# Counting the result's store on a semaphore outside the Tile context

## The chip, the cores and the metric

The kernel runs on one core of a Trainium2 chip. The metric is device microseconds of one execution; the runs of the kernel before gave 377.08, 377.2 and 377.08 us, so the median is 377.08 us. One execution was recorded by the profiler. It took 377.07 us itself; the span that the profile covers, from the first instruction to the last, is 375.3 us of that.

Engine names are those of the profile: PE is TensorE, PEld its weight loads, DVE VectorE, ACT ScalarE, POOL GpSimd, SP SyncE. A name with a q behind it (SPq, POOLq) is that engine's instruction queue, where semaphore and DMA-issuing instructions run.

## The reference

Two input rows `x` of 512 numbers are normalised, and three things are added: the row itself, sliding attention over the last 2048 keys and values of a cache of 32 heads, and a bilinear gated layer. Cut to what matters:

```
xn = layernorm(x)                                   # x: 2 x 1 x 512
q  = xn @ wq                                        # 32 heads of 128
k, v = k_cache[:, :, 6144:, :], v_cache[:, :, 6144:, :]
p  = softmax(q @ k^T / sqrt(128))                   # 2 x 32 x 1 x 2048
a  = (p @ v) @ wo                                   # 2 x 512
b  = ((xn @ w_gate) * (xn @ w_up)) @ w_down         # 512 -> 1376 -> 512
return x + a + b
```

Everything is float32. The kernel returns one tile of 128 x 128 numbers, which are the 2 x 512 results in rows 0, 1, 32, 33, 64, 65, 96 and 97; the other rows hold nothing that is read.

## The kernel before, in words

All inputs are packed on the host into one long array, `stream`, in the order in which the kernel wants them. The Sync engine pulls it in pieces of up to 31 x 512 numbers a partition into three rotating buffers named `step`; a buffer is asked for again when its last field was used. The keys of a head are multiplied by the query and summed on DVE (`products`, `sums`), the softmax is made with ACT and POOL (`maxima`, `weights`, `reciprocals`), and PE multiplies probabilities by values (`weigh`) and the outcome by `wo` (`project_o`). The gated layer's products (`project_gu`, `gate`, `down`) are spread between the heads. All of it adds up in one PSUM tile, `acc`.

Each engine's instructions are kept in the order in which the code issues them (the class `InOrder` ties each to the one before it on its engine); the Tile context inserts the semaphores. Each DMA that the context sees is counted on one of eight semaphores in turn, DMAHW0 to DMAHW7, and before a semaphore is used again the queue waits for its previous count.

The end of the program is what the change touches. After the last multiplication of `down_half`, DVE copies `acc` to the SBUF tile `o_out` (L591), and Sync stores `o_out` to DRAM (L593). Then the `with` statement of L692 ends, and the Tile context closes. In the built program its closing consists of these steps, all with line L692 in the profile:

- On Sync, five waits, each for two semaphores, which together hold every DMA semaphore and those of DVE and ACT at their last values, then a drain that waits for POOL's. The fourth of the five holds DMAHW6, on which the store counts, at 64.
- A first barrier over all five engines: PE, DVE, ACT and Sync each drain and count up one semaphore, POOL waits for four counts and then raises a second semaphore, for which each of the four waits.
- On POOL, a drain and one instruction that clears the context's twelve semaphores.
- A second barrier of the same form. Nothing of the kernel's stands behind it.

PE, DVE, ACT and POOL issue their first drain as soon as their own work is done, and stand there until Sync has come through its waits.

`PADS` sets two tiles that nothing reads or writes. They only shift the addresses of the others.

Of the kernel before, what the change touches and what calls it, by code (L numbers as in the profile page):

```python
# [8 lines left out]
F32 = mybir.dt.float32  # L9
# [7 lines left out]
P = 128  # L17
# [12 lines left out]
OUT = P  # L30
# [15 lines left out]
TG = [(0, 5), (32, 3), (32 + 3 * OWN, 1)]  # L46
TR = [OWN, OWN, FT - 8 * OWN]
TP = TG[-1][0] + TR[-1]
PADS = 608, 248


def k(h):
# [94 lines left out]
def kernel(  # L147
# [2 lines left out]
    tail: bass.AP,  # L150
    stream: bass.AP,
    out: bass.AP,
):
    nc = tc.nc
    pe, dve, act, sp = (InOrder(tc, e) for e in (nc.tensor, nc.vector, nc.scalar, nc.sync))
# [3 lines left out]
    const = ctx.enter_context(tc.tile_pool(name="const", bufs=1))  # L159
# [5 lines left out]

    const.tile([P, PADS[0]], F32, name="pad0")
    wd_tail = const.tile([TP, D], F32, name="wd_tail")
# [61 lines left out]
    acc, acc_g = acc_t[:M, :], acc_t[:, :P]  # L229
# [173 lines left out]
    def project_o(h):  # L403
        wo = got["wo", h][0]
        if h < HF:
            pe.matmul(acc, oT.pop(h), wo, start=(h == 0), stop=False)
        else:
            accumulate(oT.pop(h), wo)
        done("wo", h)
# [66 lines left out]
    def down_half(c, n):  # L476
        w = got["wh", (c, n)][0]
        for g in range(4):
            pe.matmul(
                acc_g[32 * g : 32 * g + M, n * HP : (n + 1) * HP], hT[:, c % 4, c // 4, :],  # L480
                w[:, g * HP : (g + 1) * HP], start=False, stop=(c, n) == (NFC - 1, 1),
            )
        done("wh", (c, n))
# [99 lines left out]
    project_o(H - 1)  # L583
    down(3)
    project_o(H - 2)
    o_out = const.tile([P, P], F32, name="o_out")
    const.tile([P, PADS[1]], F32, name="pad1")
    for c in range(WD[-1][1], NFC):
        for n in range(2):
            down_half(c, n)  # L590
    dve.tensor_copy(o_out, acc_g)  # L591

    sp.dma_start(out, o_out[:OUT, :])  # L593


def laid_out(x):
# [100 lines left out]
```

## Time and profile before

| what | value |
|---|---|
| median of the runs | 377.08 us |
| the profiled execution's own time | 377.07 us |
| its span, first to last instruction | 375.3 us |
| DVE busy | 294.5 us, 78% |
| PE busy | 256.5 us, 68% |
| HBM read | 159.47 MB |
| DMA, share of the chain that ended last | 60% |
| last copy, `o_out` from `acc`, begins | 372.53 us |
| store of `o_out` issued | 372.85 us |

The last row but one and the last place the change: everything that it touches lies in the 2.4 us between the issue of the store and the end of the span. The view by line of the profile gives the instructions of L692, the closing of the context, with durations in ns and the first and last start in us. The time outside the span, 377.07 less 375.3, is not covered by any record of an instruction.

### The profile page before, as it was taken

What the parts mean: (1) busy time and instruction counts of PE and PEld (TensorE: products, weight loads), DVE (VectorE), ACT (ScalarE), POOL (GpSimd) and SP (SyncE); (2) the same over time, 40 slices, a digit from 0 to 9 for tenths busy, and PEclk for the clock granted to TensorE, in tenths of its full rate; (3) what the DMA queues carried; (4) which work ended last, traced back from release to release, by engine and by line L of the source; (5) the groups of instructions that cost most, each with busy time, mean ns of one, the idle gap of its engine ahead of it and who ended that gap; (6) DMA issues with size and microseconds to landing.
All of it is one profiled execution on the core that took longest, in us unless ns stands there. A gap on an engine that the chain in (4) does not pass through costs nothing.

```text
span 375.3 us, 2897 instructions
## 1 busy us (share of the span) xinstructions
PE 256.5 (68%) x1108; PEld 89.7 (24%) x1108; DVE 294.5 (78%) x144; ACT 57.4 (15%) x260; POOL 25.6 (7%) x75
## 2 busy tenths in 40 slices
PE   3167695884586852685858805887546757699996
PEld 3133122231222220222222202222111212133343
DVE  3069999369989369999269999794699999999750
ACT  1002011110210210021012002111100211112131
POOL 1000000000000000000000000010000001000010
PEclk9999897888586996689868965898865988689899
DMA  8999999999999999999999999999999999999995
GB/s 344 419 438 479 452 407 440 433 433 434 435 427 433 433 433 433 435 426 433 433 433 436 440 433 433 447 436 420 433 440 433 435 433 433 433 433 407 419 415 230
DMA packets 4088, 159.70 MB, mean 426 GB/s; under 512 B 458, under 2 KB 714, under 8 KB 1132
## 3 DMA queue, kind: packets, MB, share of 16 engines
q1 hardware_dynamic: 4076, 159.54, 98.5%
q8 instruction: 8, 0.13, 0.1%
q14 instruction: 4, 0.03, 0.0%
HBM read 159.47 MB, written 0.07 MB: 425 GB/s over the span
## 4 chain that ended last, share of the span: by engine, by line
DMA 60%; PE 23%; DVE 14%; ACT 1%; issue 1%; SPq 0%; DVEq 0%
DMA step<-in_stream_dram 60%; PE o_ps L131 8%; DVE s L131 7%; DVE step L131 7%; PE q L131 7%; PE acc L131 5%; PE tr L131 3%; ACT o_sb L131 1%; ACT oT L131 0%; DVE m L131 0%; SPq L131 0%; DVE o_out L131 0%; DVE rec L131 0%; DVEq L131 0%
## 5 line engine op out<-in xcount | busy, mean ns | idle before, releaser
L131 DVE TENSOR_TENSOR step<-step,q 128x4096 f32<-128x4096 f32 x31 | 136.8, 4412 | 44.5 <-DMA step<-in_stream_dram 41.0
L131 DVE TENSOR_REDUCE s<-step 128x32 f32<-128x4096 f32 x32 | 141.4, 4419 | 1.1
L131 PE MATMUL o_ps<-step,p 128*16 128x512 f32 x512 | 77.7, 665 | 44.8 <-DMA step<-in_stream_dram 44.8
L131 PE MATMUL q<-step,xnb 128*128 128x512 f32 (+1 forms) x128 | 76.9, 748 | 33.9 <-DMA step<-in_stream_dram 33.9
L131 PEld LDWEIGHTS q<-step,xnb 128*128 128x128 f32 x128 | 29.3, 247 | 85.1 <-issue 69.2
L131 PE MATMUL acc<-step,oT 128*2 128x512 f32 (+1 forms) x88 | 38.0, 591 | 8.6 <-ACT oT L131 8.6
L131 PE MATMUL tr<-first,o_sb 128*128 128x2 f32 (+4 forms) x192 | 28.7, 268 | 17.1 <-ACT o_sb L131 11.8
L131 PEld LDWEIGHTS o_ps<-step,p 128*16 128x16 f32 x512 | 14.1, 100 | 96.6 <-DMA step<-in_stream_dram 53.7
L131 PEld LDWEIGHTS tr<-first,o_sb 128*128 128x128 f32 (+2 forms) x192 | 26.0, 208 | 42.4 <-ACT o_sb L131 35.0
L131 ACT COPY o_sb<-o_ps 128x512 f32<-128x512 f32 x23 | 13.5, 586 | 144.5 <-PE o_ps L131 144.5
L328 POOL PARTITION_ALL_REDUCE mm<-m x32 | 11.4, 357 | 242.9 <-DVE rec L131 137.6
L131 ACT ACTIVATE nm<-mm 128x2 f32<-128x2 f32 x32 | 6.6, 205 | 129.1 <-POOL mm L328 129.1
L131 ACT ACTIVATE p<-s,nm 128x16 f32<-128x16 f32 x64 | 19.2, 300 | 1.0
L344 POOL PARTITION_ALL_REDUCE sum<-rs x32 | 12.7, 398 | 94.7 <-ACT p L131 94.7
L131 PE MATMUL o_ps<-step,xn 128*2 128x512 f32 (+1 forms) x48 | 13.5, 618 | 5.6 <-DMA step<-in_stream_dram 5.6
L131 ACT ACTIVATE oT<-tr,rec 128x1 f32<-128x1 f32 x64 | 12.1, 260 | 26.9 <-PE tr L131 26.9
L131 DVE TENSOR_TENSOR step<-step,tr 128x4096 f32<-128x4096 f32 x1 | 4.4, 4420 | 15.0 <-DMA step<-in_stream_dram 15.0
L131 ACT ACTIVATION_READ_ACCUMULATOR p<-s,nm 128x1 f32 x64 | 11.9, 187 | 0.0
L131 PE MATMUL q<-xnb,mean_w 128*128 128x512 f32 (+4 forms) x26 | 11.5, 553 | 0.0
L131 PEld LDWEIGHTS acc<-step,oT 128*2 128x2 f32 x88 | 4.4, 88 | 22.0 <-ACT oT L131 12.1
L131 DVE RECIPROCAL rec<-sum 128x2 f32<-128x2 f32 x32 | 5.0, 155 | 4.3 <-POOL sum L344 4.3
L131 DVE COPY o_out<-acc 128x128 f32<-128x128 f32 x1 | 0.3, 292 | 8.5 <-PE acc L131 8.5
(42 smaller groups left out, 49.6 us busy)
## 6 DMA issues: line engine op xcount, KB each, us to landing
step<-in_stream_dram SPq DMA_DIRECT2D x15, 7936.0 KB, 35.5
step<-in_stream_dram SPq DMA_DIRECT2D x1, 7808.0 KB, 38.8
step<-in_stream_dram SPq DMA_DIRECT2D x1, 7680.0 KB, 20.9
step<-in_stream_dram SPq DMA_DIRECT2D x1, 7552.0 KB, 57.2
step<-in_stream_dram SPq DMA_DIRECT2D x1, 4864.0 KB
step<-in_stream_dram SPq DMA_DIRECT2D x1, 3328.0 KB, 18.9
step<-in_stream_dram SPq DMA_DIRECT2D x1, 2304.0 KB, 24.0
step<-in_stream_dram SPq DMA_DIRECT2D x2, 1024.0 KB, 16.2
```

The lines of the kernel that those rows point to most:

```text
L131: made = call(*args, **kwargs)
L328: nc.gpsimd.partition_all_reduce(mm, m, P, bass_isa.ReduceOp.max)
L344: nc.gpsimd.partition_all_reduce(sum_t[h], rs, P, bass_isa.ReduceOp.add)
```

## The change

The tile `o_out` is taken outside the Tile context, by the plain SBUF allocator, and lies at another address; the two pads are resized by 128 numbers each, so that every other tile keeps its address. The store keeps its place behind the copy by a dependency that is added by hand, is taken out of the context's own counting, and counts on a semaphore of its own, `stored`. The context's closing therefore no longer holds the store; its wait for DMAHW6 goes to 48, the count of the DMA before. Behind the closing, Sync waits for `stored` to reach 16 and clears it. In the built program these two are one instruction, a clear that carries the wait.

```diff
-PADS = 608, 248
+PADS = 480, 376
...
-    o_out = const.tile([P, P], F32, name="o_out")
     const.tile([P, PADS[1]], F32, name="pad1")
...
-    dve.tensor_copy(o_out, acc_g)
-
-    sp.dma_start(out, o_out[:OUT, :])
+    last = dve.tensor_copy(o_out, acc_g)
+    store = sp.dma_start(out, o_out)
+    tc.add_manual_dep(
+        store.ins, last.ins.name,
+        mybir.DependencyInfo(mybir.DependencyClass.Sync, mybir.DependencyReason.DATA),
+        reason="the result",
+    )
+    tc.no_tile_sem_insts.add(store.ins.name)
+    store.then_inc(stored, 16)
...
+    o_out = nc.alloc_sbuf_tensor("o_out", [P, P], F32).ap()
+    stored = nc.alloc_semaphore("stored")
     with _tile.TileContext(nc) as tc:
-        tile_sliding_attention_plus_glu_kernel(tc, *args)
+        tile_sliding_attention_plus_glu_kernel(tc, *args, o_out, stored)
+    nc.sync.wait_ge(stored, 16)
+    nc.sync.sem_clear(stored)
```

On PE, DVE, ACT and POOL every instruction and every wait stands where it stood. On Sync, the piece of the difference at the end of the program is this (`out_dram` is the result, the names in brackets are the semaphores waited for since the row before, and waits without an instruction of their own are gathered into the next row):

```order
 L131 DMA step<-in_stream_dram 128x512
 L131 DMA step<-in_stream_dram 128x256
-L131 DMA out_dram<-o_out 128x128 [waits DMAHW6_49,DVE_49]
-L692 UNCONDITIONAL_BRANCH
+L131 DMA out_dram<-o_out 128x128 [waits DVE_49]
+L701 UNCONDITIONAL_BRANCH
+L704 ISA [waits DMAHW3_49,DMAHW2_49,DMAHW4_49,DMAHW1_49,DMAHW5_49,DMAHW0_49,DMAHW6_49,DVE_49,DMAHW7_49,Activation_49,Pool_49,barrier_Pool_Activation_PE_DVE_SP_release,stored]
```

The store lost its wait for DMAHW6, the closing lost none of its waits, and one instruction, the clear with its wait for `stored`, stands behind the closing's last barrier. With the wait that went and the clear that came, Sync has 68 instructions in both programs.

More of the change, by code (lines that the diff above doesn't have):

```diff
@@ L152 @@
     out: bass.AP,
+    o_out: bass.AP,
+    stored,
 ):
@@ L691 @@
         args.append(nc.dram_tensor(f"out_{i}_dram", shape, dt, kind="ExternalOutput").ap())
+    o_out = nc.alloc_sbuf_tensor("o_out", [P, P], F32).ap()
+    stored = nc.alloc_semaphore("stored")
     with _tile.TileContext(nc) as tc:
-        kernel(tc, *args)
+        kernel(tc, *args, o_out, stored)
+    nc.sync.wait_ge(stored, 16)
+    nc.sync.sem_clear(stored)
     r = _run(nc, [arrays], core_ids=[0])
```

## The prediction

> **What bounds the kernel, and what of it the change can reach.** I read the page first, for the shape of the whole.
>
> ```profile
> span 375.3 us, 2897 instructions
> DMA  8999999999999999999999999999999999999995
> q1 hardware_dynamic: 4076, 159.54, 98.5%
> DMA 60%; PE 23%; DVE 14%; ACT 1%; issue 1%; SPq 0%; DVEq 0%
> ```
>
> The DMA engines are busy nine tenths of nearly every slice and hold 60% of the chain that ended last. The loading of keys and values bounds the kernel, and only the last slice thins out. None of that is touched, since all five engines run the same instructions in the same order up to the store. So the question is what happens in the last slice. The instructions in order of time show how it ends:
>
> ```profile
> 371.83 0.63 PE L131 MATMUL acc<-step,hT 128*2 128x64 f32 x32
> 372.53 0.29 DVE L131 COPY o_out<-acc 128x128 f32<-128x128 f32 x1 [8.53 <-PE acc L131]
> 372.85 0.35 SPq L131 DMA_DIRECT2D out_dram<-o_out  x1
> ```
>
> PE ends, DVE copies, Sync issues the store at 372.85, and no engine computes any more. What Sync waits for from 372 us on is told by the view of its own waits (us in total, times, longest):
>
> ```profile
> SPq L131 <- DVE o_out L131: 18.0, 1, 18.0
> SPq L692 <- DMA out_dram<-o_out: 1.0, 1, 1.0
> SPq L692 <- PEq L692: 0.6, 2, 0.4
> ```
>
> In the closing (L692) Sync stands 1.0 us for the store to land, and then 0.6 us in two waits of the barriers. So the closing is paid behind the store. I cut the end into stretches at the instants found below, from the store's issue to the span's end (length, then busy time and count of PE, PEld, DVE, ACT, POOL, then clock, DMA share, GB/s):
>
> ```profile
> 372.85:373.20 0.35, 0.00 (x0) 0.00 (x0) 0.00 (x0) 0.00 (x0) 0.00 (x0) 1.00 0.00 0
> 373.20:373.69 0.49, 0.00 (x0) 0.00 (x0) 0.00 (x0) 0.00 (x0) 0.00 (x0) 1.00 0.00 0
> 373.69:374.05 0.36, 0.00 (x0) 0.00 (x0) 0.00 (x0) 0.00 (x0) 0.00 (x0) 1.00 0.60 182
> 374.05:374.40 0.35, 0.00 (x0) 0.00 (x0) 0.00 (x0) 0.00 (x0) 0.00 (x0) 1.00 0.00 0
> 374.40:375.28 0.88, 0.00 (x0) 0.00 (x0) 0.00 (x0) 0.00 (x0) 0.00 (x0) 0.71 0.00 0
> ```
>
> The store is issued in 0.35 us, 0.49 us pass before its first packets, these move for 0.36 us, and 0.35 us more pass before Sync sees the count, 1.55 us in all. Then 0.88 us of closing follow.
>
> The instants come from the instructions of L692 (counts, then ns least/median/most, first and last start). The first row is Sync's from 373.2 to 373.45; the second is Sync's from 373.4 to 374.42; the rest are all engines' from 374.75 on:
>
> ```profile
> L692 SPq EVENT_SEMAPHORE  x3: 28/28/28, 373.2 to 373.4; - x3
> ...
> L692 SPq EVENT_SEMAPHORE  x1: 27/27/27, 374.4 to 374.4; - x1
> ...
> L692 POOLq DRAIN  x2: 34/58/82, 374.8 to 375.0; - x2
> ...
> L692 POOLq EVENT_SEMAPHORE_RANGE_CLEAR  x1: 96/96/96, 374.9 to 374.9; - x1
> ...
> L692 SPq EVENT_SEMAPHORE  x1: 17/17/17, 375.2 to 375.2; - x1
> ...
> L692 PEldq EVENT_SEMAPHORE  x1: 51/51/51, 375.2 to 375.2; - x1
> ```
>
> Three of Sync's five closing waits pass at once; in windows of 0.02 to 0.03 us the first lies at 373.25 and the third at 373.38, so they follow each other by about 0.065 us. The fourth, which holds the store, runs only at 374.40 (it alone lies between 374.39 and 374.41). Sync leaves the last barrier in a row of 17 ns that lies at 375.21 to 375.24, and PE in the row of 51 ns, in which the span ends: it is the only one of L692 running at 375.27 and none is left at 375.285, so I put the end at 375.28.
>
> **The change part by part.**
>
> 1. The store's wait for DMAHW6 goes. Sync stood 18.0 us there for DVE's copy (the first row of its waits), so the earlier wait passed inside that time. Worth nothing; without that cover it would be one passed wait, 0.03 to 0.065 us by the rows above. The copy is still what the store waits for, so the issue stays at 372.85.
>
> 2. `o_out` has another address. No row shows this copy or store at two addresses. The nearest are POOL's first fills, two of one shape at two addresses:
>
> ```profile
> L678 POOL MEMSET const-float32-0.0<- x1: 98/98/98, 0.2 to 0.2; 128x1 f32 x1
> L678 POOL MEMSET const-float32-1.0<- x1: 99/99/99, 0.3 to 0.3; 128x1 f32 x1
> ```
>
> They differ by 1 ns of 98, which on the copy's 0.29 us and the store's 0.36 us of packets is under 0.01 us, to either side. I take nothing. The pads hold every other tile in place.
>
> 3. The closing no longer waits for the store. Its fourth wait passes about 0.065 us behind the third, at 373.45 instead of 374.40, which is 0.95 us earlier (the row of waits says 1.0). All that follows it, 0.88 us, moves by as much: the last barrier ends at 375.28 - 0.95 = 374.33, and Sync is through it at 375.24 - 0.95 = 374.29. The other four engines wait for Sync alone there: each came to its first drain when its work was done, DVE with its copy last of all, by the row of its two drains in the closing (the first from 372.5, 330 ns long):
>
> ```profile
> L692 DVEq DRAIN  x2: 19/174/330, 372.5 to 374.9; - x2
> ```
>
>
> 4. Behind the closing Sync waits for `stored`. The store is seen at 374.40 as before, for nothing of its 1.55 us changes. Sync is there 0.11 us early, so the store and not the closing ends last. That is the new wait: nothing is queued behind it on Sync but the end of the program, and no other engine waits for it. If the closing took 0.11 us longer than here, the cover would be gone and each further 0.1 us would be paid.
>
> 5. The clear of `stored` is new on the path. No row shows a clear on Sync. The same instruction on POOL took 0.096 us for twelve semaphores; Sync's plain semaphore instruction in the same place took 0.017 us. It clears one semaphore, so it lies between the two, and I take the middle, 0.06 us. The dearest instruction that Sync has here, the issue of the store, took 0.35 us, and is the far end.
>
> The sum: 374.40 + 0.06 = 374.46 for the end of the span, against 375.28, a gain of 0.82 us. The ends by the nearer rows are 0.86 us (0.017) and 0.78 us (0.096), by the far one 0.53 us. The profiled execution took 377.07 us, so 376.25; the median of the runs is 0.01 above it, which gives 376.26 us, or 0.22% less. The bound above which a measurement of this kernel tells a change from none is 0.2%, 0.75 us, so the forecast clears it by 0.07 us only.
>
> This assumes that the 1.79 us outside the span (377.07 - 375.28) stay as they are and begin when the last engine is through. No row shows what happens in them. The Trainium skill, page "Runtime: NRT & Kernel Launch", section "The ~15µs preamble/postamble breakdown", says that after the kernel there is first a barrier that waits for all engines, of about 1.5 us, and only then the resetting of semaphores; by that rule Sync's late clear sets the end and the gain is the 0.82 us of the sum. The page's stages behind the kernel add up to about 5 us, which is more than the 1.79 us that this case leaves for all that is outside, so I don't take it as settled.
>
> **The rivals.**
>
> *Only four engines count.* If what follows the span begins on each engine by itself and Sync is not the one that it ends on, Sync's 0.11 us of waiting and its clear are hidden, and the gain is the whole shift of part 3, 0.95 us: 376.13 us. For it speaks that four engines of five are released at 374.33; against it, that all five left the barrier together before, so nothing shows which one is waited for.
>
> *The new end is dearer.* The clear on Sync costs as much as the dearest row, 0.35 us: the span ends at 374.75, the gain is 0.53 us, and the time is 376.55 us, no change that can be told. The same comes of 0.29 us more anywhere between the landing and the end. For it speaks that POOL's clear took more than five times its plain semaphore instruction, with a drain of its own ahead; against it, that Sync's drains and waits all took 7 to 28 ns. It decides from a clear of 0.13 us on (0.82 - 0.75 + 0.06).
>
> *Slower: the added instruction is not at hand.* The clear stands behind the place at which Sync's program ended. Were it to be fetched from memory when Sync comes to it, at 374.29, the fetch would stand bare. Its price is bounded by these rows, the fetches by their queue (packets, MB, share of 16 engines) and the first load of the kernel (KB, us from issue to landing):
>
> ```profile
> q8 instruction: 8, 0.13, 0.1%
> ...
> first<-in_stream_dram SPq DMA_DIRECT2D x1, 271.0 KB, 2.9
> ```
>
> A packet of instructions took about 0.001 x 16 x 375.3 / 8 = 0.75 us of one engine; a whole load took 2.9 us. With 2.9 us the span ends at 374.29 + 2.9 + 0.06 = 377.25 and the time is 379.04 us. It turns slower from a fetch of 0.93 us on (375.28 - 374.29 - 0.06), and by 0.2% from 1.68 us. Against it: Sync has 68 instructions before and after, and before, it passed its whole closing in steps of 0.065 us with no hole but the store's.
>
> That the change does not do what it says is not open: in the built program the closing's wait for DMAHW6 is at 48 now, the count before the store's.
>
> **How the numbers follow.** The likeliest is the sum, 0.58, with its own range from 376.15 to 376.40: the two nearer ends, 376.22 and 376.30, widened by the 0.1 us by which the runs before differ (377.08 to 377.2). Only four engines count: 0.18. A dearer end: 0.20, spread between 376.33 and 376.7. The fetch: 0.04. The range 376.05 to 376.60 holds the first two and most of the third. Faster by over 0.2% means under 376.33: all of the second and 0.50 of the first, since its margin of 0.07 us is less than the scatter of the runs: 0.68. Within 0.2%: the other 0.08 of the first and the third, 0.28. Slower: the fetch, 0.04.
>
> **What would show it.** In the changed kernel's profile: up to the store's issue at 372.85 nothing moves by more than runs do. Part 3 is right if Sync's five closing waits follow each other without the hole of 1.0 us, and the other engines' last rows of the closing lie near 374.3. Part 4 is right if Sync's waits name the store once more, behind the closing, with some 0.1 us. Part 5 is right if a clear on Sync of 20 to 100 ns ends the span at 374.4 to 374.5. If the span shrinks by 0.82 us and the time by another amount, the assumption on what lies outside is wrong. What would make the forecast wrong most easily is a store that lands later than 374.40: nothing covers it now, and each 0.1 us of it goes to the end as it did before.

## The result, and the profile after

The changed kernel takes 376.12 us (median of 10 runs, 376.03 to 376.30), the kernel before 377.12 us beside it (10 runs, 376.92 to 377.26). The ratio is 0.9974, with a 95% interval from 0.9964 to 0.9983: faster by 1.00 us of the medians, about a quarter of a percent. Forecast were 376.26 us and a gain of 0.82 us, within 376.05 to 376.60. The profiled execution took 376.18 us itself.

The page of the changed kernel has as many instructions as before, the same queue of loads and the same chain:

```profile
span 374.5 us, 2897 instructions
q1 hardware_dynamic: 4076, 159.54, 98.7%
DMA 60%; PE 23%; DVE 14%; ACT 1%; issue 1%; SPq 0%; DVEq 0%
```

The end in order of time, and then Sync's waits from 370 us on:

```profile
372.61 0.29 DVE L131 COPY o_out<-acc 128x128 f32<-128x128 f32 x1 [8.53 <-PE acc L131]
372.93 0.35 SPq L131 DMA_DIRECT2D out_dram<-o_out  x1
```

```profile
SPq L131 <- DVE o_out L131: 18.1, 1, 18.1
SPq L701 <- PEq L701: 0.6, 2, 0.4
```

The copy and the issue take what they took, 0.29 and 0.35 us, and come 0.08 us later than in the profile of before, less than the 0.34 us by which the runs of the kernel before differ here (376.92 to 377.26). The row of 1.0 us in which the closing waited for the store is gone. The closing's instructions (L701 now), in the view by line, are the same in number, and within 10 ns in length:

```profile
L701 SPq EVENT_SEMAPHORE  x7: 17/28/28, 373.3 to 374.3; - x7
L701 PEldq EVENT_SEMAPHORE  x2: 51/51/51, 373.9 to 374.3; - x2
L701 POOLq EVENT_SEMAPHORE_RANGE_CLEAR  x1: 96/96/96, 374.0 to 374.0; - x1
```

In the part from 373.2 to 373.7 us Sync's five closing waits now stand together, where before the fourth was at 374.4:

```profile
L701 SPq EVENT_SEMAPHORE  x5: 28/28/28, 373.3 to 373.6; - x5
```

And the new instruction, the clear on Sync that carries the wait for `stored`, in the view of its line:

```profile
L704 SPq EVENT_SEMAPHORE_RANGE_CLEAR  x1: 30/30/30, 374.5 to 374.5; - x1
```

The same stretches as before, cut at this profile's instants (issue; to the last packet; to the end of the wait for `stored`; the clear):

```profile
372.93:373.28 0.35, 0.00 (x0) 0.00 (x0) 0.00 (x0) 0.00 (x0) 0.00 (x0) 1.00 0.00 0
373.28:374.12 0.84, 0.00 (x0) 0.00 (x0) 0.00 (x0) 0.00 (x0) 0.00 (x0) 1.00 0.27 78
374.12:374.49 0.37, 0.00 (x0) 0.00 (x0) 0.00 (x0) 0.00 (x0) 0.00 (x0) 1.00 0.00 0
374.49:374.52 0.03, 0.00 (x0) 0.00 (x0) 0.00 (x0) 0.00 (x0) 0.00 (x0) 1.00 0.00 0
```

The store takes 1.56 us from issue to seen (1.55 before), then 0.03 us of clear follow in the place of 0.88 us of closing. From the store's issue to the end of the span there were 375.28 - 372.85 = 2.43 us, and there are 1.59 us now: 0.84 us less, where the sum had 0.82. PE's last row of the closing ends at 374.40 (found in a narrow window, as before), 0.12 us ahead of the span's end.

One number does not fit the sum. The time less the span was 1.80 us on average over 35 runs of the kernel before (each run lists its span to 0.1 us), and is 1.70 us over these 10 runs. A tenth of a microsecond was gained where no instruction is recorded. That is what most of the experiments are about.

### The profile page after: what moved, and what is told of

Read it like the earlier page. It is cut to its first block, busy times and chain, and to the rows that moved or that the text cites. A ratio compares the mean times of both kernels' runs of the same rounds, so it can differ in the third digit from the quotient of the medians.

```text
span 374.5 us, 2897 instructions
## 1 busy us (share of the span) xinstructions
PE 260.7 (70%) x1108; PEld 90.3 (24%) x1108; DVE 294.5 (79%) x144; ACT 57.2 (15%) x260; POOL 25.6 (7%) x75
## 4 chain that ended last, share of the span: by engine, by line
DMA 60%; PE 23%; DVE 14%; ACT 1%; issue 1%; SPq 0%; DVEq 0%
DMA step<-in_stream_dram 60%; PE o_ps L131 8%; DVE s L131 7%; DVE step L131 7%; PE q L131 7%; PE acc L131 5%; PE tr L131 3%; ACT o_sb L131 1%; ACT oT L131 0%; DVE m L131 0%; SPq L131 0%; DVE o_out L131 0%; DVE rec L131 0%; DVEq L131 0%
## 5 line engine op out<-in xcount | busy, mean ns | idle before, releaser
L131 PE MATMUL q<-step,xnb 128*128 128x512 f32 (+1 forms) x128 | 78.7, 763 | 35.4 <-DMA step<-in_stream_dram 35.4
L131 PE MATMUL acc<-step,oT 128*2 128x512 f32 (+1 forms) x88 | 39.7, 612 | 8.6 <-ACT oT L131 8.6
```

What stands on the lines that cost most here:

```text
L131: made = call(*args, **kwargs)
```

## The experiments

All are edits of the changed kernel, timed beside the kernel before. The time less the span is called *the rest* from here on; its mean over a kernel's runs repeats to about 0.02 us from session to session: it was 1.78 to 1.80 us for the kernel before in the three sessions of these experiments, and 1.70 and 1.68 us for the changed kernel in two.

**The address alone.** The store goes back to the context's counting; the tile stays outside.

```diff
-    tc.no_tile_sem_insts.add(store.ins.name)
-    store.then_inc(stored, 16)
...
-    nc.sync.wait_ge(stored, 16)
-    nc.sync.sem_clear(stored)
```

> The tile o_out lies outside the context and the pads are resized, as in the changed kernel, but the store counts on the context's own semaphore again and nothing waits behind the closing. Theory (the gain comes of the closing running beside the store): the closing waits for the store again, Sync stands about 1.0 us in its fourth wait, and the time is that of the kernel before, 377.1 us within 0.1. Rival (the address of o_out or the pads give part of the gain): 376.1 to 376.9 us, with a shorter copy or store.

Measured: 377.18 us, a ratio of 0.9998 (0.9990 to 1.0007) to the kernel before. Sync's waits have the store again:

```profile
SPq L698 <- DMA out_dram<-o_out: 1.0, 1, 1.0
```

So the address and the pads give nothing, and the whole gain hangs on where the store is waited for.

**Sync ends later.** Sixteen clears of an unused semaphore on Sync, behind its clear of `stored`. The semaphore `idle` is added in the same way in the other runs with clears.

```diff
+    idle = nc.alloc_semaphore("idle")
...
     nc.sync.sem_clear(stored)
+    for _ in range(16):
+        nc.sync.sem_clear(idle)
```

> The changed kernel with 16 more clears of an unused semaphore on Sync behind its clear of stored; at about 0.065 us each, the step of Sync's closing waits, Sync ends 1.0 us later, span 375.5 us. Theory of the sum (what lies outside the span begins when the last engine is through): the whole of it is paid, 377.1 to 377.2 us, and time less span stays at 1.7 us. Rival (only four engines count, Sync has slack outside the span): less is paid than the span grows, so that time less span falls; with a slack of 0.5 us 376.6 us, with one of 1.0 us or more 376.1 us.

Measured: 377.28 us. The clears in the view of their line:

```profile
L707 SPq EVENT_SEMAPHORE_RANGE_CLEAR  x16: 25/30/49, 374.5 to 375.9; - x16
```

The span is 376.0 us, 1.5 us longer than the changed kernel's, and the time rose by 1.16 us from its 376.12. The rest fell from 1.70 to 1.31 us. Four tenths of Sync's lateness were not paid: Sync has a slack outside the span, and the assumption that what follows begins with the last engine is wrong for Sync. (Part of the 1.31 us may be a transfer behind the span, of which more below; the next run has none.)

**Sync ends a little later.** The same with four clears, small enough to fit into that slack.

```diff
     nc.sync.sem_clear(stored)
+    for _ in range(4):
+        nc.sync.sem_clear(idle)
```

> The changed kernel with 4 more clears on Sync, 0.06 us each as the 16 of the earlier run, so that Sync ends at 374.75 and with it the span. New theory (Sync has slack outside the span: the time is the later of the other engines' end, 374.40, plus 1.80 us, and of Sync's end plus 1.31 us): the first is 376.20, the second 376.06, so the time does not move from the changed kernel's 376.12 us by more than 0.1, and time less span falls to 1.45 us. Rival (the last engine's end counts, with 1.70 us outside): 376.4 us, time less span 1.7 us.

Measured: 376.26 us, the span 374.8 us, the rest 1.44 us. The clears end the span 0.25 us behind where it would have ended:

```profile
L705 SPq EVENT_SEMAPHORE_RANGE_CLEAR  x1: 30/30/30, 374.5 to 374.5; - x1
L707 SPq EVENT_SEMAPHORE_RANGE_CLEAR  x4: 25/28/39, 374.6 to 374.8; - x4
```

The rest fell by 0.26 us, as much as the clears took. The median lies 0.14 us over the changed kernel's first measurement, a little more than the 0.1 us expected, and 0.04 us over its second (376.22 us, below). On the kernel before in the same session (377.17 us) it gains 0.91 us, where the changed kernel gained 1.00 and 0.93 us: so the clears cost 0.02 to 0.09 us, against the 0.25 us that they would have had to. The rival's 376.4 us and 1.70 us did not come. This small lateness of Sync costs nothing that can be told from the scatter.

**Another barrier.** One more barrier of all engines between the closing and the wait.

```diff
+    nc.all_engine_barrier()
     nc.sync.wait_ge(stored, 16)
```

> The changed kernel with one more barrier of all engines between the closing and Sync's wait for stored. A barrier of the closing took 0.33 to 0.48 us there. Theory (the store ends last, with the closing's end 0.1 to 0.15 us ahead of it): the cover is used up and only the rest is paid, 0.2 to 0.35 us: span 374.7 to 374.9, 376.3 to 376.5 us, and Sync no longer waits for stored. Rival (the closing ended last, or its cover is larger): all of it, 376.45 to 376.6 us, or nothing, 376.1 us.

Measured: 376.61 us, the rest 1.79 us. Sync's waits and PE's row of the new barrier:

```profile
SPq L703 <- PEq L703: 0.3, 1, 0.3
...
L703 PEldq EVENT_SEMAPHORE  x1: 51/51/51, 374.8 to 374.8; - x1
```

The barrier moved the end on PE from 1.47 to 1.80 us behind the store's issue (374.40 - 372.93 and 374.80 - 373.01), by 0.33 us, and the span's end by 0.24 us only, as the cover of part 4 has it. The gain on the kernel before in the same session (377.20 us) is 0.59 us, where the changed kernel's was 1.00 and 0.93 us, so the barrier cost 0.34 to 0.41 us. It went to where the rival had it: the barrier is paid whole, as the 0.33 us on PE have it and not as the 0.24 us of the span, since the end of the closing counts and not that of the store.

**The other engines later.** The sixteen clears on PE, ACT, DVE and POOL in turn.

```diff
     nc.sync.sem_clear(stored)
+    for _ in range(16):
+        nc.tensor.sem_clear(idle)      # nc.scalar, nc.vector, nc.gpsimd
```

> The changed kernel with the same 16 clears on PE, behind its last barrier, where it is free about 0.12 us before Sync. At 0.065 to 0.1 us each PE ends 0.9 to 1.5 us behind Sync, span 375.4 to 376.0 us. Theory of the sum: the whole growth of the span is paid and time less span stays at 1.7 us, 377.0 to 377.6 us. Rival (engines are not alike in what follows the span): time less span differs from that of the run with the clears on Sync by 0.1 us or more.

> The changed kernel with 16 clears of an unused semaphore on ACT behind its last barrier, about 0.06 us each, so that ACT ends near 375.4. If ACT is waited for as PE is, time less span is 1.7 to 1.8 us and the time 377.1 to 377.2 us. If ACT has a slack as Sync has, 376.7 us or less.

> The same with the 16 clears on DVE, 0.06 to 0.08 us each, so that DVE ends at 375.4 to 375.7. If DVE is waited for as PE is, time less span is 1.7 to 1.8 us and the time 377.1 to 377.5 us. If it has a slack as Sync has, 0.5 us less than that.

> The changed kernel with 16 clears of an unused semaphore on POOL behind its last barrier, about 0.1 us each with what lies between them, so that POOL ends at 375.5 to 376.2. If POOL is waited for as ACT is (time less span 1.75 us there), the time is 377.2 to 378.0 us. If it has a slack as DVE (0.4 us) and Sync (0.5 us) have, time less span is 1.3 to 1.4 us.

The last clears, by the views of their lines in the four profiles, PE, ACT, DVE and POOL:

```profile
L707 PEldq EVENT_SEMAPHORE_RANGE_CLEAR  x16: 56/56/63, 374.4 to 376.2; - x16
```

```profile
L707 ACTq EVENT_SEMAPHORE_RANGE_CLEAR  x16: 41/41/41, 374.6 to 375.6; - x16
```

```profile
L707 DVEq EVENT_SEMAPHORE_RANGE_CLEAR  x16: 55/55/55, 374.4 to 375.7; - x16
```

```profile
L707 POOLq EVENT_SEMAPHORE_RANGE_CLEAR  x16: 44/44/44, 374.7 to 375.8; - x16
```

| engine that ends last | time, us | the rest, us |
|---|---|---|
| POOL | 377.29 | 1.85 |
| ACT | 377.22 | 1.75 |
| PE | 378.17 | 1.70 |
| DVE | 377.19 | 1.40 |
| Sync | 377.28 | 1.31 |

The rest depends on which engine is late: a late DVE leaves 0.45 us less behind it than a late POOL, a late Sync 0.54 us less. For Sync, PE and ACT this has to be read with care. In the profiles of these three runs, and in no other of this case, DMA moved something behind the span, within the time that the rest covers. This is PE's, in the view by stretch (the last two numbers are the DMA share and GB/s):

```profile
377.20:378.20 1.00, 0.00 (x0) 0.00 (x0) 0.00 (x0) 0.00 (x0) 0.00 (x0) 0.50 0.06 16
```

With Sync late 14 GB/s moved from 376.40 to 377.00 us, with ACT late the same from 376.60 to 377.20 us; in the traces each is one packet of 8 to 16 KB on a queue named instruction. What it adds to the time is not shown. So DVE's slack against POOL is shown without it, and Sync's by the four clears (0.25 us); that ACT and PE are waited for at once is likely, not shown. PE's 378.17 us lies above the 377.0 to 377.6 us expected: its clears began every 0.12 us, not every 0.065 to 0.1 us. Its mean also hides a spread from 1.56 to 1.91 us between runs, with spans from 376.2 to 376.8 us, for which no cause was found.

**The store from ACT's queue.** If the closing's end counts, it pays to start the closing earlier. Sync's 0.35 us of issuing stand ahead of its five waits; ACT has nothing to do there.

```diff
-    store = sp.dma_start(out, o_out)
+    store = act.dma_start(out, o_out)
```

> The changed kernel with the store issued from ACT's queue instead of Sync's. Sync no longer issues for 0.35 us ahead of its five closing waits, so the waits pass beside ACT's issue and the closing starts about 0.45 us earlier. New theory: the other engines are through at 373.95, plus 1.80 us gives 375.75; Sync's wait for the store ends as before at 374.5, plus 1.31 us gives 375.83; so 375.8 us, and the span stays at 374.5 us. Rival (the last engine's end counts): the store still ends the span, nothing changes, 376.1 us. A first DMA on ACT's queue may cost something that no row shows, which would lift both.

Measured: 375.99 us (5 runs), the rest 1.45 us. The direction is the new theory's, but less than its 375.8 us. To compare within one session, the changed kernel and this one were run again side by side:

> The changed kernel as it is, beside the next run on the same chip. Both theories: 376.1 to 376.2 us, time less span 1.70 us.

> The kernel with the store issued from ACT's queue once more, to be compared with the changed kernel in the same session. Its profile had the other engines through the closing at 374.24 and the store seen at 374.55. New theory: 374.24 + 1.80 = 376.04 us and 374.59 + 1.31 = 375.90 us, the later counts, with the end of the copy 0.05 us later there than in the changed kernel's profile: 0.1 to 0.2 us under the changed kernel. Rival (the store ends both): the same as the changed kernel within 0.05 us.

Measured: 376.22 us (9 runs, rest 1.68 us) for the changed kernel, a ratio of 0.9966 (0.9955 to 0.9978; by the medians 0.9975, a gain of 0.93 us on 377.15 us), and 375.96 us (7 runs, rest 1.43 us) for the store from ACT, 0.9963 (0.9949 to 0.9978). The second profile of the store from ACT, the issue of the store, its wait on Sync, ACT's drains and PE's last row, and the clear:

```profile
372.75 0.38 ACTq L131 DMA_DIRECT2D out_dram<-o_out  x1
...
SPq L704 <- DMA out_dram<-o_out: 0.4, 1, 0.4
...
L701 ACTq DRAIN  x2: 8/80/152, 373.2 to 373.6; - x2
...
L701 PEldq EVENT_SEMAPHORE  x1: 51/51/51, 374.0 to 374.0; - x1
...
L704 SPq EVENT_SEMAPHORE_RANGE_CLEAR  x1: 30/30/30, 374.4 to 374.4; - x1
```

The closing ends at 374.01, 1.26 us behind the issue at 372.75, against 1.47 us in the changed kernel. It won 0.21 us instead of the 0.45 expected, because ACT issues in 0.38 us and then drains for 0.152 us, and the barrier waits for that. Sync now stands 0.4 us for the store, which ends the span as before, and the time fell all the same. By the medians this is the fastest of the kernels, by 0.13 us over two sessions and by 0.26 us side by side, where 0.1 to 0.2 us were expected; the intervals of the two ratios overlap, so that it is faster than the changed kernel is likely and not shown.

**What fits all of them.** The closing's end on PE (the end of its row of 51 ns, from narrow windows) beside the time of the same profiled execution:

| kernel | closing's end on PE | span | time | time less closing's end |
|---|---|---|---|---|
| before | 375.28 | 375.3 | 377.07 | 1.79 |
| changed | 374.40 | 374.5 | 376.18 | 1.78 |
| changed, again | 374.45 | 374.6 | 376.24 | 1.79 |
| address alone | 375.18 | 375.2 | 376.96 | 1.78 |
| four clears on Sync | 374.45 | 374.8 | 376.26 | 1.81 |
| another barrier | 374.80 | 374.8 | 376.64 | 1.84 |
| store from ACT | 374.24 | 374.6 | 376.06 | 1.82 |
| store from ACT, again | 374.01 | 374.4 | 375.80 | 1.79 |

Time less span goes from 1.4 to 1.8 us in these rows; time less the closing's end stays within 1.78 to 1.84 us, and in none of these profiles did DMA move anything behind the span. So the time here is set by the end of the closing, and Sync's end decides only where it comes so late that its own 1.31 us (or less, if the transfer is part of them) reach further. In the changed kernel that is 374.52 + 1.31 = 375.83, 0.35 us short of the 376.18 measured. Which engine's end of the closing is the one that is waited for, these rows can't tell: in every profile the last rows of the five engines end within 0.09 us of each other, PE's last.

## Why the prediction was right, and where it was off

- *Part 1, the store's wait for DMAHW6 is worth nothing.* As put: Sync still stood 18.1 us there for the copy.
- *Part 2, the address costs nothing.* Shown by the address alone: a ratio of 0.9998, and copy and issue as long as before.
- *Part 3, the closing moves by 0.95 us.* Right. Behind the issue it ended at 375.28 - 372.85 = 2.43 us and ends at 1.47 us, 0.96 us earlier.
- *Part 4, the store ends last, with a cover of 0.11 us.* Right for the span: PE's row ends 0.12 us ahead of it. But the view of waits does not name the store behind the closing as I said it would; the wait is carried by the clear, and 0.1 us left no row. In the store from ACT, where it was 0.4 us, the row is there.
- *Part 5, a clear of 0.06 us on Sync.* It took 0.030 us, nearer to the plain semaphore instruction's 0.017 than to POOL's 0.096, which clears twelve. The term was 0.03 us too large.
- *The sum, 0.82 us.* For the span it is right: 0.84 us behind the issue.
- *The assumption that the 1.79 us outside the span stay and begin when the last engine is through.* This is the step that failed. The four clears and the sixteen on Sync show that Sync's end is not what the time follows; the wait for the store and its clear lie beside something that takes longer. The change gained the whole shift of part 3 and not that shift less the store's tail: 0.96 us in the two profiles, 1.00 us in the medians and 0.93 us when it was measured again. What was listed as a rival with 0.18, *only four engines count*, 376.13 us, is what happened, against 376.12 us measured. Its name is too simple: DVE has such a slack as well, by the table of late engines. The prediction's last warning, that each 0.1 us of a later landing goes to the end, fell with the same step: the four clears kept Sync 0.25 us longer, and of that 0.02 to 0.09 us was paid.

The range held because it reached to that rival. The sum's own range, 376.15 to 376.40 us, did not hold the 376.12 us; by its own working (376.22 less 0.1) its lower end should have been 376.12. That the measured time fell within 0.01 us of the rival's 376.13 us is luck: only 0.13 us lie between the two forecasts, and measured again the changed kernel took 376.22 us. What tells the two mechanisms apart is the rest and the rows above, not the median.

The Trainium skill's page "Runtime: NRT & Kernel Launch" (section "The ~15µs preamble/postamble breakdown") has a barrier that waits for all engines right behind the kernel. By that rule the gain would have been the span's 0.84 us. The runs don't bear it out in this simple form: whatever waits there, a late Sync or DVE reaches it with 0.4 to 0.5 us to spare.

- *The rival of a dearer end* fell with the clear of 0.030 us. *The rival of the fetch* did not occur in the changed kernel, whose clear ran as soon as the store was seen. Something like it was seen where more was added: of the sixteen clears on Sync, twelve lie before 375.3 us, one at 375.33 us and the last three from 375.8 us on, and between 375.37 and 375.79 no clear is running:

```profile
L707 SPq EVENT_SEMAPHORE_RANGE_CLEAR  x12: 25/30/49, 374.5 to 375.2; - x12
...
L707 SPq EVENT_SEMAPHORE_RANGE_CLEAR  x3: 25/30/31, 375.8 to 375.9; - x3
```

What Sync stood for in these 0.4 us is not shown: between 375.36 and 375.80 us no DMA moved anything (share 0.00, 0 GB/s), so no transfer of instructions lies in the hole, and its cause stays open.

## What to carry to other kernels

The Tile context's closing (its waits, two barriers, one clear: 0.88 us here) runs behind the last store unless the store is taken out of what it waits for; a wait for the store behind the closing adds to the span only what the store takes longer than the closing, and on Sync that did not even add to the time here. Before paying attention to the last instruction of the span, compare the time with the ends of the single engines over several variants: here time less the closing's end stayed within 0.06 us, while time less span went from 1.4 to 1.8 us. Once the closing is what counts, the next gain lies in what holds it up, such as the issue of the store on the engine that also walks through the closing's waits (likely worth 0.13 to 0.26 us here, not shown).

## What was not expected of the hardware

- An engine that ends late is not paid alike: with sixteen clears added on it, POOL, ACT and PE left 1.85, 1.75 and 1.70 us behind the span, DVE 1.40 and Sync 1.31 us; ACT's, PE's and Sync's may hold a transfer as well.
- A clear of one semaphore took 25 to 30 ns on Sync for most of the sixteen, 41 ns on ACT, 44 ns on POOL, 55 ns on DVE and 56 ns on PE; the clear of twelve on POOL took 96 ns.
- A drain on ACT right behind a DMA issue took 152 ns, where ACT's other drain in that closing took 8 ns.
